# Attention of a two-layer fused kernel: both batch rows of a chunk in every operation

## The chip, the cores and the metric

One NeuronCore of a Trainium2 chip runs the whole program. The metric is the time of one execution on the device in microseconds (us); lower is better. Engines as they are named here: PE is TensorE's matrix products (PEld its weight loads), DVE is VectorE, ACT is ScalarE, POOL is GpSimd, SP is SyncE, which issues all transfers.

## What is computed

An mLSTM-like attention over 2 batch rows, 8 heads, 768 tokens and 40 channels a head; its result, 1536 tokens by 320, goes through two feed-forward layers of 2048 channels with different nonlinearities. All in fp32.

```python
for t in range(S):
    kt, vt, qt = (k[:, :, t], v[:, :, t], q[:, :, t])
    m_new = np.maximum(f_gate[:, :, t] + m, i_gate[:, :, t])
    f_stab = np.exp(f_gate[:, :, t] + m - m_new)
    i_stab = np.exp(i_gate[:, :, t] - m_new)
    m = m_new
    C = f_stab[:, :, None, None] * C + i_stab[:, :, None, None] * np.einsum('bhd,bhe->bhde', vt, kt)
    n = f_stab[:, :, None] * n + i_stab[:, :, None] * kt
    h_tilde = np.einsum('bhde,bhe->bhd', C, qt)
    denom = np.maximum(np.abs(np.einsum('bhd,bhd->bh', n, qt)[:, :, None]), 1.0)
    y[:, :, t] = 1.0 / (1.0 + np.exp(-o_gate[:, :, t])) * h_tilde / denom
x = y.transpose(0, 2, 1, 3).reshape(B * S, H * D)
h = x @ moe_w_in;   x = (h * np.clip(h + 3.0, 0.0, 6.0) / 6.0) @ moe_w_out
h = x @ moe2_w_in;  out = (h * np.tanh(np.log1p(np.exp(h)))) @ moe2_w_out
```

## The kernel before

The 768 tokens are cut into 6 chunks of 128. A *unit* is one batch row of one chunk; there are 12. For each unit `loads` brings q and k (`qke`, 416 KB) and k, v and the output gate (`kvo`, 484 KB); `scores` makes the products of q and k (tile `s`); `decays` makes the decay matrix by a scan (tile `fb`) and multiplies it with `s`; `values` scales v with the input gate and takes the gate's sigmoid; `cross` multiplies q with the carried state (`x`) and scales it into `oc`; `carry` scales k, multiplies it with v (`st`) and updates the state `c`; `within` multiplies `fb` with v (`z`, for both rows of a chunk together); the rest of `unit` adds `z` and `oc`, divides, gates, transposes (`xp`) and writes the result to X as a high part (`xh`) and a low part (`xl`). The products of attention use small tiles of the array, 40 or 64 rows by 64 columns; many stand side by side, and one run of them in PE's list is called a group below. The other products use the whole array.

Layer 1 takes the first two chunks in steps of 256 tokens (`ph`, `acc`) and the other four in blocks of 512 (`phw`, `accw`); layer 2 takes three blocks of 512 (`qh`, `bcc`). Every fp32 product is split into high and low parts. The weights arrive as `ri` and `ro` (768 and 640 KB for each of the 8 slots of a layer) and are split in `prep` by ACT and DVE or POOL; three of the `ro` slots of layer 1 have their low part made by PE instead (`low_on_pe`, tile `pw`). Until layer 1 has begun, `keep_warm` fills PE's idle time with products of zeros (`pz`).

The order on every engine is written out when the program is built: each job is a generator that asks for an engine with a duration, `Flow` plays them against one another with modelled durations and the table `P` of priorities, and the engines then run their lists in that order, each waiting in place for what an instruction needs. So an instruction that is late holds all behind it on its engine. SP's list of transfers is such a list too.

Of the kernel before, what the change touches and what calls it, by code (L numbers as in the profile page):

```python
# [8 lines left out]
F32 = mybir.dt.float32  # L9
F32R = mybir.dt.float32r  # L10
# [27 lines left out]
KVO = 2 * DM + H * E1  # L38
# [4 lines left out]
    "const": [21, 95, 223],  # L43
    "gates": [27, 37, 26, 68, 145, 320],
    "load": [17, 51, 194, 1, 24, 30, 176, 184, 28, 55, 116, 316],
    "score": [110, 40, 164, 39, 262, 141, 186, 143, 25, 248, 107, 242],
    "value": [92, 232, 149, 93, 334, 34, 284, 175, 138, 309, 342, 269],
    "carry": [330, 64, 56, 180, 231, 13, 133, 4, 229, 307, 62, 8],
    "unit": [89, 79, 57, 136, 46, 102, 70, 52, 42, 20, 169, 237],
# [8 lines left out]
    ],  # L58
    "down2": [
        244, 204, 112, 163, 183, 32, 155, 14, 78, 91, 19, 222, 33, 294, 0, 109, 29, 125, 99, 105, 211, 47,  # L60
        72, 83, 171, 63, 11, 142, 6, 202, 101, 310, 185, 77, 53, 111, 217, 224, 103, 9, 86, 22, 12, 208,
        270, 170, 333, 158,
    ],
    "wide1": [
        2, 258, 123, 289, 199, 159, 311, 61, 331, 255, 139, 167, 165, 279, 197, 131, 150, 195, 326, 118,
        250, 45, 246, 282, 203, 339, 302, 286, 278, 303, 329, 35,
    ],
    "down1w": [
        38, 193, 220, 264, 221, 7, 153, 295, 214, 124, 177, 156, 69, 65, 67, 74, 5, 36, 104, 84, 31, 117,
        114, 100, 82, 260, 73, 179, 80, 18, 173, 328,  # L70
    ],
    "drain": [59, 272, 129, 243, 43, 10, 54, 227, 238, 182],
    "now": [15, 16],
    "window": [0.05],
    "on_value": [0, 1, 1, 0, 1, 1, 2, 1, 1, 2, 1, 1],
    "on_key": [0, 0, 1, 2, 1, 0, 1, 2, 0, 2, 1, 1],
    "on_gate": [1, 0, 0, 0, 0, 2, 2, 0, 1, 2, 1, 0],
    "pool_state": [1, 0, 0, 1, 0, 1, 1, 0, 0, 0, 0, 0, 0, 0, 0, 0, 0, 0, 1, 0],
# [4 lines left out]
        0, 0, 0, 0, 0, 0, 0, 1, 0, 0, 1, 0, 1, 1, 1, 1, 1, 0, 0, 0, 0, 1, 1, 1, 1, 0, 0, 1, 0, 0, 0, 0, 1,  # L83
        0, 0, 0, 0, 0, 0, 0, 1, 1, 0, 0, 0, 1, 1, 0,
# [3 lines left out]
    "pe_low": [0, 1, 0, 0, 0, 0, 0, 0, 0, 0, 0, 0],  # L88
    "spread": [1, 1, 0, 0, 0, 0],
    "decay": [189, 134, 290, 137, 144, 308, 325, 283, 174, 120, 96, 313],  # L90
    "gload": [257, 178, 198, 48, 90, 298, 201, 41, 148, 287, 98, 128],
    "cross": [196, 162, 296, 172, 66, 200, 50, 181, 267, 241, 280, 2],
    "within": [315, 140, 317, 3, 304, 230],
    "on_cross": [0, 0, 0, 0, 0, 0, 0, 0, 0, 1, 0, 0],
# [7 lines left out]
FBS = 4  # L102


def make_consts():
    import numpy as np

    c = np.zeros((B * H, CW), np.float32)
    for r in range(B * H):
        b, h = divmod(r, H)  # L110
        p, g = divmod(h, 4)
        c[r, 64 * p : 64 * p + D] = 1.0
        c[r, CM + b * 4 + g] = 1.0
    return c
# [27 lines left out]
class Flow:  # L142
# [5 lines left out]
    TICK, COLUMNS = 10.24 / 3, 4000  # L148

# [85 lines left out]
    def transfer(self, place, t, size, n, issue):  # L235

        rate = 15e3 if t < 10 else 18.5e3
        for i in range(n):
            self.rings[i] = max(self.rings[i], t + 1.0) + size / n / rate
        end = max(self.rings[:n]) + 0.25  # L240
# [57 lines left out]
def mlstm_mlp_kernel(ctx, tc, qk, kvon, gates_io, w1i, w1o, w2i, w2o, eyes, consts, out):  # L298
# [21 lines left out]
    apool = att_stack.enter_context(tc.tile_pool(name="apool", bufs=2))  # L320
# [10 lines left out]
    in_fb, in_qke, in_kvo, in_rc, in_gp, in_fz, in_pr = (Slots(n) for n in (FBS, 2, 2, 2, 1, 1, 1))  # L331
    in_oc = [Slots(2), Slots(1)]
# [106 lines left out]
    for j in range(len(BLOCKS)):  # L439
        X.append((xpool.tile([128, 3, 512], F32R, tag=f"xh{j}", name=f"xh{j}"),  # L440
                  xpool.tile([128, 3, 512], F32R, tag=f"xl{j}", name=f"xl{j}")))
# [222 lines left out]
    def gates(c):  # L664
# [49 lines left out]
        yield PE, 0.25, 40  # L714
        T.matmul(pf[:QP, 256:272], cst[:, 0:QP], dd.rearrange("r g a -> r (g a)"), start=True, stop=True, skip_group_check=True)
        T.matmul(pf[:, 272:280], pr, ident[:16, 0:8], start=True, stop=True, skip_group_check=True)
        for a in range(2):
            T.matmul(pf[64 - 64 * a : 128 - 64 * a, 280:288], pr[:, a * HL : (a + 1) * HL], ident[:16, 8:16],
# [4 lines left out]
        yield DVE, 0.07  # L723
        V.tensor_copy(prefix[c], pf[:, 272:288])
        yield DVE, 0.07
# [625 lines left out]
```

## Time and profile before

| | |
|---|---|
| median of 3 runs | 444.06 us (443.64 to 445.39) |
| the profiled execution, its own time | 446.41 us |
| its span, first to last instruction | 444.6 us |
| busy: PE, DVE, ACT, POOL | 433.0, 303.4, 282.6, 67.6 us |
| instructions: DVE, ACT, POOL | 598, 552, 67 |
| moved by the transfers | 39.28 MB |

The span and what lies around it (1.8 us) make the profiled execution's own time, and this was 2.35 us over the median of the runs. PE's busy time counts overlapping products whole and counts the products of zeros, so a busy PE is not a useful one: below, the time of a product is read from its start to the start of the next.

### The profile page before, as it was taken

The numbers are of one execution on the slowest core, as the hardware profiler recorded it, in microseconds if no ns is written. First come the engines' busy times: TensorE is split into PE (matmuls) and PEld (weight loads), VectorE is DVE, ScalarE is ACT, GpSimd is POOL, SyncE is SP. The second block draws the span as 40 slices with busy tenths as digits, with TensorE's granted clock in tenths as the row PEclk, the third lists the DMA queues.
The fourth block names the chain that finished last, engine by engine and source line by source line (L and its number), as shares of the span: only waits on it lengthen the run. The fifth ranks groups of instructions, "written<-read, shape, count | busy, mean of one in ns | idle before, by whom it ended". The sixth has DMA issues, their size and how long they took to land.

```text
span 444.6 us, 9247 instructions
## 1 busy us (share of the span) xinstructions
PE 433.0 (97%) x3768; PEld 373.0 (84%) x3768; DVE 303.4 (68%) x598; ACT 282.6 (64%) x552; POOL 67.6 (15%) x67
## 2 busy tenths in 40 slices
PE   7999998999999999999999999999999999999995
PEld 5778797999997787888788888999998998989994
DVE  3889999797476653658786537766656666566674
ACT  3358785449358444369778448766767666666763
POOL 2114004534211025101325010000000000000000
PEclk9999999899999999999999999999999999999998
DMA  7957759344131328007352000000020000100002
GB/s 212 329 167 234 242 192 306 83 136 131 39 93 45 88 68 310 1 9 260 135 161 99 1 0 2 0 1 0 0 60 1 1 0 1 53 8 0 2 0 59
DMA packets 12118, 39.28 MB, mean 88 GB/s; under 512 B 2444, under 2 KB 4140, under 8 KB 12076
## 3 DMA queue, kind: packets, MB, share of 16 engines
q1 hardware_dynamic: 12076, 38.70, 27.3%
q8 instruction: 29, 0.48, 0.5%
q14 instruction: 13, 0.11, 0.1%
HBM read 36.46 MB, written 2.23 MB: 87 GB/s over the span
## 4 chain that ended last, share of the span: by engine, by line
PE 80%; DVE 7%; ACT 6%; DMA 3%; issue 1%; SPq 0%; ACTq 0%; DVEq 0%
PE qh L457 15%; PE accw L474 14%; PE phw L457 13%; PE acc L474 7%; PE ph L457 6%; PE bcc L1155 5%; PE bcc L1154 5%; PE bcc L1153 5%; PE pz L1186 2%; PE s L813 2%; DVE u L1098 2%; PE z L983 1%; PE x L894 1%; DMA ro<-in_w1o 1%; PE st L945 1%; ACT u L1100 1%
## 5 line engine op out<-in xcount | busy, mean ns | idle before, releaser
L1155 PE MATMUL bcc<-wd,gl 128*128 128x320 f32 x192 | 59.6, 311 | 0.5 <-DVE gl L1110 0.5
L1153 PE MATMUL bcc<-wd,gh 128*128 128x320 f32 x192 | 59.5, 310 | 0.1
L1154 PE MATMUL bcc<-wd,gh 128*128 128x320 f32 x192 | 59.3, 309 | 0.0
L457 PE MATMUL qh<-xl,wh 128*128 128x512 f32 x144 | 56.6, 393 | 0.0
L457 PE MATMUL qh<-xh,wh 128*128 128x512 f32 x144 | 56.5, 392 | 0.0
L1104 DVE SCALAR_TENSOR_TENSOR u<-u,qh 128x512 f32<-128x512 f32 (+1 forms) x49 | 33.1, 675 | 33.4 <-ACT u L1102 33.4
L1100 ACT ACTIVATE u<-u,two 128x512 f32<-128x512 f32 (+1 forms) x49 | 35.0, 715 | 31.8 <-DVE u L1098 31.8
L474 PE MATMUL accw<-ghw,wd 128*128 128x512 f32 x160 | 53.8, 401 | 0.0
L541 DVE SCALAR_TENSOR_TENSOR rw<-rw,phw 128x512 f32<-128x512 f32 x32 | 21.9, 685 | 24.3 <-ACT rw L539 24.2
L1153 PEld LDWEIGHTS bcc<-wd,gh 128*128 128x128 f32 x192 | 36.1, 188 | 2.8 <-ACT gh L1108 0.9
L1110 DVE SCALAR_TENSOR_TENSOR gl<-u,gh 128x512 fp32r<-128x512 f32 (+1 forms) x49 | 33.1, 675 | 7.8 <-ACT gh L1108 7.7
L474 PE MATMUL accw<-glw,wd 128*128 128x512 f32 x96 | 38.1, 397 | 0.0
L457 PE MATMUL phw<-xh,wh 128*128 128x512 f32 x96 | 37.9, 395 | 0.0
L457 PE MATMUL qh<-xh,wl 128*128 128x512 f32 x96 | 37.9, 394 | 0.0
L457 PE MATMUL phw<-xl,wh 128*128 128x512 f32 x96 | 37.6, 392 | 0.0
L1154 PEld LDWEIGHTS bcc<-wd,gh 128*128 128x128 f32 x192 | 36.1, 188 | 1.8
L1094 ACT ACTIVATE u<-qh 128x512 f32<-128x512 f32 (+1 forms) x49 | 28.5, 584 | 14.0 <-PE qh L457 14.0
L1155 PEld LDWEIGHTS bcc<-wd,gl 128*128 128x128 f32 x192 | 36.1, 188 | 1.3 <-DVE gl L1110 1.3
L474 PEld LDWEIGHTS accw<-ghw,wd 128*128 128x128 f32 x160 | 29.4, 188 | 6.5
L1098 DVE SCALAR_TENSOR_TENSOR u<-u 128x512 f32<-128x512 f32 (+1 forms) x49 | 33.4, 681 | 1.6
L474 PE MATMUL acc<-gh,wd 128*128 128x256 f32 x160 | 34.4, 298 | 0.0
L539 ACT ACTIVATE rw<-phw,half 128x512 f32<-128x512 f32 x32 | 22.0, 688 | 18.5 <-PE phw L457 17.9
(163 smaller groups left out, 994.8 us busy)
## 6 DMA issues: line engine op xcount, KB each, us to landing
ri<-in_w1i SPq DMA_DIRECT2D x8, 768.0 KB, 8.6
ri<-in_w2i SPq DMA_DIRECT2D x8, 768.0 KB, 8.7
kvo<-in_kvon SPq DMA_DIRECT2D x12, 484.0 KB, 5.3
ro<-in_w1o SPq DMA_DIRECT2D x8, 640.0 KB, 10.9
ro<-in_w2o SPq DMA_DIRECT2D x8, 640.0 KB, 5.8
qke<-in_qk SPq DMA_DIRECT2D x12, 416.0 KB
fb<-fzd SPq DMA_DIRECT2D x8, 256.0 KB, 3.4
out<-ot SPq DMA_DIRECT2D x6, 160.0 KB, 1.9
```

Source lines behind the costliest of these rows:

```text
L457: T.matmul(ph, a, b, start=(i == 0), stop=(i == len(seq) - 1))
L474: T.matmul(acc[k], a, b, start=start, stop=stop, skip_group_check=True)
L539: A.activation(r, ph, AF.Relu, bias=half, scale=1.0 / 6.0)
L541: V.scalar_tensor_tensor(out=r, in0=r, scalar=1.0, in1=ph, op0=ALU.min, op1=ALU.mult)
L1094: A.activation(u, ph, AF.Exp)
L1098: V.scalar_tensor_tensor(out=u, in0=u, scalar=2.0, in1=u, op0=ALU.add, op1=ALU.mult)
L1100: A.activation(u, u, AF.Ln, bias=two)
L1104: V.scalar_tensor_tensor(out=u, in0=u, scalar=0.5, in1=ph, op0=ALU.subtract, op1=ALU.mult)
L1110: V.scalar_tensor_tensor(out=gl, in0=u, scalar=-2.0, in1=gh.bitcast(F32), op0=ALU.mult, op1=ALU.subtract)
L1153: T.matmul(acc, a, hi, start=st, stop=False)
L1154: T.matmul(acc, a, lo, start=False, stop=False)
L1155: T.matmul(acc, b, hi, start=False, stop=sp)
```

## The change

A chunk's two rows are handled together. The host lays the inputs out by chunk, with the 16 heads of both rows side by side; `loads` brings one `qke` (832 KB) and one `kvo` (968 KB) a chunk; `scores`, `carry` and `cross` each issue the products of both rows in one group; the elementwise operations take 16 heads in one instruction (8 where a tile of PSUM ends). Buffers: `qke` and `kvo` have one slot each in place of two (chunks 1 and 3 keep their `kvo` in the space of the third X tile), `fb` has two of double width, and `oc` one. `scaled` now uses DVE or POOL, no longer ACT. Table `P` is new throughout, and `Flow`'s model of a transfer has other constants. The counts of products, of feed-forward instructions and of bytes stay the same.

```diff
-KVO = 2 * DM + H * E1
+KVO = B * (2 * DM + H * E1)
...
-    "score": [110, 40, 164, 39, 262, 141, 186, 143, 25, 248, 107, 242],
+    "score": [9, 84, 243, 262, 211, 292],
...
-FBS = 4
+FBS = 2
+R = B * H
...
-    apool = att_stack.enter_context(tc.tile_pool(name="apool", bufs=2))
+    apool = att_stack.enter_context(tc.tile_pool(name="apool", bufs=1))
...
-    in_fb, in_qke, in_kvo, in_rc, in_gp, in_fz, in_pr = (Slots(n) for n in (FBS, 2, 2, 2, 1, 1, 1))
-    in_oc = [Slots(2), Slots(1)]
+    in_fb, in_qke, in_kvo, in_x2, in_oc, in_gp, in_fz, in_pr = (Slots(n) for n in (FBS, 1, 1, 1, 1, 1, 1, 1))
...
+        t["qke"] = apool.tile([QP, B, 2, 4, L], F32, tag="qke", name=f"qke{c}")
+        yield SP, 852e3, ev["qk"], 13, 0.54
+        SY.dma_start(out=t["qke"], in_=qk[c])
+        t["ring"] = in_x2 if c in (1, 3) else in_kvo
+        yield t["ring"]
...
+        yield SP, 992e3, ev["kvo"]
+        SY.dma_start(out=kvo[:, 0:KVO], in_=kvon[c * L : (c + 1) * L])
...
+    def scaled(on, x, scale, n):
+        yield flow.elementwise(on, 0.07 + R * n / 960, R * n)
+        tt(G if on else V, x, x, scale.unsqueeze(2).to_broadcast([128, R, n]), ALU.mult)
+
+    def quads(first=0):
+        for a in range(first, 2):
+            for p in range(2):
+                yield a, slice(a * HL, (a + 1) * HL), p, slice(64 * p, 64 * p + D)
+
+    def scores(c):
...
+        yield PE, 0.95, 2048, 1
+        for b in range(B):
+            for h in range(4):
+                cols = slice((b * 4 + h) * HL, (b * 4 + h + 1) * HL)
+                for a, z, p, r in quads():
+                    x = t["qke"][r, b]
+                    T.matmul(sp[p][z, cols], x[:, 1, h, z], x[:, 0, h, z], start=True, stop=True, skip_group_check=True)
+        flow.set(done[c]["s"])
...
+        for b in range(B):
+            for h in range(4):
+                g = b * 4 + h
+                for a, z, p, r in quads(0 if c else 1):
+                    out = slice(64 * (a ^ b), 64 * (a ^ b) + 64)
+                    T.matmul(x[p][out, g * E1 : (g + 1) * E1], t["qke"][r, b, 0, h, z], states[2 * c + a][r, g, :],
+                             start=True, stop=True, skip_group_check=True)
+        flow.set(done[c]["cross"])
...
+        yield done[c]["s"]
+        flow.put(in_qke)
...
+        yield PE, 0.95, 1312, 1
+        for b in range(B):
+            for h in range(4):
+                g = b * 4 + h
+                for p in range(2):
+                    r = p * 8 + g
+                    w = QP - 64 if p else 64
+                    for a in range(n):
+                        z = slice(a * HL, (a + 1) * HL)
+                        T.matmul(sps[a][64 * p : 64 * p + w, g * E1 : (g + 1) * E1], kf[z, r * D : r * D + w], vi[z, r, :],
+                                 start=True, stop=True, skip_group_check=True)
...
```

What the change does to the order is seen at three places. SP's list begins, before, with the gates and the inputs of chunk 0 row by row (`qke_0`, `kvo_0`, two of each):

```order
L1170 DMA gio<-in_gates_io 16x2x128
L1172 DMA eye<-in_eyes 128x256
L762 DMA qke_0_120<-in_qk 104x1024
L1226 DMA cst<-in_consts 16x112
L769 DMA kvo_0_168<-in_kvon 128x968
L354 DMA ro_0_156<-in_w1o 128x2560
L762 DMA qke_0_176<-in_qk 104x1024
L354 DMA ri_0_157<-in_w1i 128x3072
L769 DMA kvo_0_185<-in_kvon 128x968
```

and now with four weight loads ahead of them:

```order
L357 DMA ro_1_137<-in_w1o 128x2560
L1184 DMA gio<-in_gates_io 16x2x128
L1186 DMA eye<-in_eyes 128x256
L1244 DMA gio<-in_gates_io 16x2x640
L1240 DMA cst<-in_consts 16x112
L357 DMA ro_3_138<-in_w1o 128x2560
L357 DMA ri_0_139<-in_w1i 128x3072
L357 DMA ro_0_140<-in_w1o 128x2560
L767 DMA qke_104<-in_qk 104x2048
L775 DMA kvo_158<-in_kvon 128x1936
```

The four weight loads moved ahead of chunk 0's inputs, and each input is one load of both rows; behind these rows the new list has `ri_2`, `ro_4`, `ro_2`, `ri_1`, then `qke` and `kvo` of chunk 1.

On PE, before, the products that make low weight parts (`pw`) stand between steps of layer 1 (here behind `ph_2`, the third of its steps):

```order
L391 MATMUL pw_3_320_861<-ro_3_603,eye 128x320
L392 MATMUL pw_3_320_861<-wd_3_141,minus 128x320
L671 MATMUL pg_893<-eye,gio 128x16
L672 MATMUL pg_893<-eye,gio 128x16
L391 MATMUL pw_4_320_901<-ro_4_738,eye 128x320
L392 MATMUL pw_4_320_901<-wd_4_138,minus 128x320
```

and now all six pairs stand ahead of layer 1's first step, among the products of zeros; four of them are these:

```order
L1200 MATMUL pz<-zeros 128x512
L394 MATMUL pw_4_320_539<-ro_4_318,eye 128x320
L395 MATMUL pw_4_320_539<-wd_4_122,minus 128x320
L394 MATMUL pw_2_320_547<-ro_2_328,eye 128x320
L395 MATMUL pw_2_320_547<-wd_2_113,minus 128x320
L1200 MATMUL pz<-zeros 128x512
L394 MATMUL pw_4_320_559<-ro_4_318,eye 128x320
L395 MATMUL pw_4_320_559<-wd_4_122,minus 128x320
L394 MATMUL pw_2_320_564<-ro_2_328,eye 128x320
L395 MATMUL pw_2_320_564<-wd_2_113,minus 128x320
```

They moved from inside layer 1 to the time before it. The last is what PE does right ahead of the first product of layer 1 (`ph_0`). Before, it is the scores of one row of chunk 1 and filling:

```order
L813 MATMUL s_1_0_582<-qke_1_364 64x64
L813 MATMUL s_1_1_583<-qke_1_364 64x64
L1186 MATMUL pz<-zeros 128x512 x2
L457 MATMUL ph_0_610<-xh_93,wh_0_127 128x256
L457 MATMUL ph_0_610<-xl_94,wh_0_127 128x256
```

Now it is chunk 1's products of k and v, of both rows, behind the scores of both:

```order
L942 MATMUL st_0_643<-kvo_532 64x41
L942 MATMUL st_1_644<-kvo_532 64x41
L942 MATMUL st_0_643<-kvo_532 40x41
L942 MATMUL st_1_644<-kvo_532 40x41
L465 MATMUL ph_0_680<-x_93,wh_0_108 128x256 x2
```

So layer 1 now begins behind all that chunk 1's `st` waits for, its `kvo` among it.

## Rows read from the trace of the kernel before


**Rows 1.** Windows by stage: us, busy time of each engine (instructions), granted clock, DMA share, GB/s.

```profile
0.00:35.10 35.10, 32.01 (x462) 24.47 (x463) 23.60 (x67) 15.83 (x34) 6.55 (x16) 1.00 0.76 239
35.10:82.20 47.10, 44.30 (x563) 39.10 (x561) 41.78 (x102) 33.77 (x82) 12.47 (x12) 0.96 0.71 232
82.20:190.00 107.80, 107.80 (x1469) 93.41 (x1469) 72.35 (x165) 59.53 (x155) 31.10 (x27) 1.00 0.31 97
190.00:444.60 254.60, 248.92 (x1280) 216.02 (x1278) 165.72 (x268) 173.52 (x283) 17.50 (x12) 1.00 0.12 37
```

**Rows 2.** Timeline around layer 1's first product: start, us, engine, line, operation.

```profile
19.18 2.35 PE L1186 MATMUL pz<-zeros 128*128 128x512 f32 x9
...
35.14 0.28 PE L457 MATMUL ph<-xh,wh 128*128 128x256 f32 x1
...
35.26 1.09 ACT L362 CAST top<-ri 128x768 f16<-128x768 bf16 x1
```

**Rows 3.** Timeline of PE at its only long wait ahead of layer 2.

```profile
72.93 0.28 PE L457 MATMUL ph<-xl,wh 128*128 128x256 f32 x1
75.18 0.69 PE L813 MATMUL s<-qke 40*64 40x64 f32 x32 [1.97 <-DVE dd L305]
```

**Rows 4.** The window behind that wait, columns as in rows 1.

```profile
77.00:80.50 3.50, 3.50 (x19) 3.28 (x17) 1.43 (x4) 1.14 (x3) 2.44 (x3) 0.51 0.82 246
```

**Rows 5.** Timeline of PE around groups of small-tile products.

```profile
88.20 0.28 PE L457 MATMUL ph<-xh,wh 128*128 128x256 f32 x1
88.32 0.28 PE L457 MATMUL ph<-xl,wh 128*128 128x256 f32 x1
88.53 0.68 PE L894 MATMUL x<-c,qke 40*64 40x41 f32 x32
89.14 0.39 PE L457 MATMUL ph<-xh,wh 128*128 128x256 f32 x1
89.36 0.28 PE L457 MATMUL ph<-xl,wh 128*128 128x256 f32 x1
...
93.00 1.14 PE L983 MATMUL z<-kvo,fb 64*64 64x41 f32 x64
94.07 0.50 PE L474 MATMUL acc<-gh,wd 128*128 128x256 f32 x2
```

**Rows 6.** Timeline of PE at one `pw` pair.

```profile
48.52 0.83 PE L391 MATMUL pw<-ro,eye 128*128 128x320 f32 x2
...
49.34 0.28 PE L457 MATMUL ph<-xh,wh 128*128 128x256 f32 x1
```

**Rows 7.** Windows of the first 40 us, columns as in rows 1.

```profile
0.00:10.00 10.00, 7.67 (x72) 5.48 (x74) 3.08 (x15) 3.49 (x10) 2.96 (x10) 1.00 0.70 208
10.00:20.00 10.00, 10.00 (x144) 7.94 (x141) 7.56 (x16) 4.61 (x8) 1.16 (x2) 1.00 1.01 338
...
30.00:40.00 10.00, 9.11 (x104) 7.79 (x101) 9.72 (x15) 7.50 (x15) 4.29 (x5) 1.00 0.81 265
```

**Rows 8.** Timeline: v of chunk 0's second row is scaled.

```profile
18.85 0.74 POOL L305 TENSOR_TENSOR kvo<-kvo,ist 128x328 f32<-128x328 f32 x1
```

**Rows 9.** DVE by line and shape: count, busy us, mean ns, idle ahead.

```profile
L305 DVE TENSOR_TENSOR fb<-fb,s 128x256 f32<-128x256 f32 x24 | 9.2, 411 | 0.2
L305 DVE TENSOR_TENSOR wl<-ri,wh 128x512 fp32r<-128x512 f32 x11 | 7.6, 688 | 0.8 <-ACT wh L402 0.6
```

**Rows 10.** Timeline of DVE: its longest wait in the second stage.

```profile
81.17 0.18 DVE L724 COPY px<-pf 128x16 f32<-128x16 f32 x1 [2.74 <-PE pf L718]
```

**Rows 11.** Transfers as the page lists them: KB each, us from issue to landing.

```profile
ri<-in_w1i SPq DMA_DIRECT2D x8, 768.0 KB, 8.6
...
kvo<-in_kvon SPq DMA_DIRECT2D x12, 484.0 KB, 5.3
ro<-in_w1o SPq DMA_DIRECT2D x8, 640.0 KB, 10.9
```

More of the change, by code (lines that the diff above doesn't have):

```diff
@@ L148 @@
     TICK, COLUMNS = 10.24 / 3, 4000
+    DMA = dict(rings0=2.0, slow=13e3, fast=20e3, until=3.0, start=1.9, end=0.5)
     def __init__(self):
@@ L235, in transfer @@
     def transfer(self, place, t, size, n, issue):
-        rate = 15e3 if t < 10 else 18.5e3
+        d = self.DMA
+        rate = d["slow"] if t < d["until"] else d["fast"]
         for i in range(n):
-            self.rings[i] = max(self.rings[i], t + 1.0) + size / n / rate
-        end = max(self.rings[:n]) + 0.25
+            self.rings[i] = max(self.rings[i], t + d["start"]) + size / n / rate
+        end = max(self.rings[:n]) + d["end"]
         self.landed.append(end)
@@ L838, in decays @@
-        yield (DVE, 1.135) if P["spread"][c] else (DVE, 1.135, True)
-        V.tensor_tensor_scan(out=f2, data0=fin, data1=ident8, initial=0.0, op0=ALU.mult, op1=ALU.add)
-        if P["spread"][c]:
-            flow.put(in_h)
-        yield ACT, 0.1
-        A.copy(t["ul"], f2.rearrange("p (h t) -> p h t", h=H)[:, :, HL - 1 : HL])
-        flow.set(done[u]["ul"])
-        yield done[u]["s"]
-        for p in range(2):
-            yield DVE, 0.33
-            part = f2[:, p * 256 : (p + 1) * 256]
-            tt(V, part, part, t["s"][p][:, 0:256], ALU.mult)
+        else:
+            yield got[c]["f"]
@@ new lines, in decays @@
+        for p in range(2):
+            part = fin = f[:, p * 512 : (p + 1) * 512]
+            if spread:
+                yield in_h
+                fin = bank(f"fb{c}_{p}")
+                yield PE, 0.95, 2048, 2
+                for r in range(8):
+                    col = istab[c][:, p * 8 + r : p * 8 + r + 1].to_broadcast([128, HL])
+                    for a in range(2):
+                        z = slice(a * HL, (a + 1) * HL)
+                        T.matmul(fin[z, r * HL : (r + 1) * HL], col, identz[:, z], start=True, stop=True, skip_group_check=True)
+            yield (DVE, 1.135) if spread else (DVE, 1.135, True)
+            V.tensor_tensor_scan(out=part, data0=fin, data1=ident8, initial=0.0, op0=ALU.mult, op1=ALU.add)
+            if spread:
+                flow.put(in_h)
@@ new lines, in mixture @@
+        port = (True,) * (2 - len(parts))
+        for o, r, _ in parts:
+            yield (DVE, 0.08) + port
+            V.tensor_scalar(out=r, in0=o[..., D : D + 1], scalar1=1.0, scalar2=None, op0=ALU.max)
+            yield (DVE, 0.08) + port
+            V.scalar_tensor_tensor(out=r, in0=o[..., D : D + 1], scalar=-1.0, in1=r, op0=ALU.mult, op1=ALU.max)
+        yield DVE, 0.17
+        V.reciprocal(out=rc, in_=rc)
+        yield from scaled(P["on_gate"][c], so, rc, D)
+        for o, _, g in parts:
+            yield (DVE, 0.74 if len(parts) == 1 else 0.41) + port
+            tt(V, g, o[..., 0:D], g, ALU.mult)
+            flow.put(in_a if port == () else in_fb)
@@ new lines, in mixture @@
+        y = so.rearrange("p (q b h) d -> p q b (h d)", q=2, b=B)
+        tail = t["tail"].rearrange("p (b x) -> p b x", b=B)
+        for x in range(2):
+            yield ACT, 0.15
+            A.copy(tail[:, :, 64 * x : 64 * x + 64].rearrange("p b (q d) -> p q b d", q=2), y[:, :, :, 128:160])
+        for b in range(B):
+            i = 2 * c + b
+            yield in_a
+            xp = bank(f"xp{b}_{c}")
+            yield PE, 0.32, 1536
+            for k, part in enumerate((y[:, 0, b, 0:128], y[:, 1, b, 0:128], tail[:, b, :])):
+                T.matmul(xp[:, k * 128 : (k + 1) * 128], part, ident, is_transpose=True, start=(k == 0), stop=(k == 2),
+                         skip_group_check=True)
+            if c // 2 == len(X):
+                yield ends[3]
+                new_x()
+            xcol = ((c % 2) * 2 + b) * L
+            xh, xl = (z[:, :, xcol : xcol + L] for z in X[c // 2])
+            ps = xp[:, 0:384].rearrange("p (k t) -> p k t", k=3)
+            yield ACT, 0.37
+            A.copy(xh, ps)
+            if P["pe_low"][i]:
+                yield have["minus"]
+                yield PE, 0.18, 384
+                T.matmul(ps, minus, xh, start=False, stop=True, skip_group_check=True)
+                yield ACT, 0.36
+                A.copy(xl, ps)
+            else:
+                yield DVE, 0.47
+                sub(xl, ps, xh.bitcast(F32))
+            flow.put(in_a)
+            flow.set(x1[c][b])
@@ L1240, in scan_rest, with after_attention @@
             yield from scan_gates(i, *SCANS[i])
-    def after_attention(waits, last):
+    def after_attention(waits):
         for e in waits:
```

481 lines of the change are left out of this document (201 added, 280 removed), and 14 rows, old and new, of the table P.

## The prediction, as put on record before the changed kernel ran

> **What bounds the kernel now.** I read the windows by stage first. From 82.2 us on PE is busy 107.80 of 107.80 us and then 248.92 of 254.60 [rows 1], at a granted clock of 1.00; the missing 5.7 us are the passage between the layers and the tail, whose order the change does not touch. Between 35.1 and 82.2 PE is busy 44.30 of 47.10 us at a clock of .96. Ahead of that its 32.01 busy us are mostly products of zeros. The timeline gives the border: the first product of layer 1 starts at 35.14, right behind filling [rows 2]. So the kernel's time is a sum of three things: when layer 1 starts, how long PE's list is from there, and what PE loses on the way. Savings on DVE, ACT or POOL count only through the first and the third.
>
> What PE loses from 35.1 to 82.2 is 2.8 us of idle time and a clock effect of 47.1 × .04 = 1.9, together 4.7. The timeline shows where: behind the product at 72.93, PE has nothing until 75.18, since it waits for DVE [rows 3], and from 77.0 to 80.5 its granted clock is .51, that is 1.2 GHz in place of 2.4 [rows 4].
>
> **PE's list from the start of layer 1.** A group of 32 small products shows its fixed cost between whole-array products [rows 5]. From one `ph` product to the next is .12 us (88.20 to 88.32). The last one ahead of the group takes .21 (to 88.53), so the entry costs .09. The first behind it takes .22 (89.14 to 89.36) and so costs .10 more. The group of 32 lasts .61 and the `z` group of 64 lasts 1.07, so 32 products cost .46 and .15 is fixed. A group that is merged into another thus saves .09 + .10 + .15 = .34. I counted the groups in both orders from layer 1's start: 32 before, 17 after. Those 15 give 5.1 us; if entry and exit were hidden by something else, the .15 alone gives 2.3. Three groups' worth of products, one of `s` and two of `st`, moved ahead of the start: 3 × .46 = 1.4. Six `pw` pairs moved ahead too; one takes .82 (48.52 to 49.34, three records) [rows 6], so 6 × .82 = 4.9. Feed-forward products are the same in number. The sum is 11.4, and 8.6 with groups at .15 each. I take 11.0, near the top, because entry and exit costs stand in plain sight around nearly every group of the trace.
>
> **The start of layer 1.** It needs chunk 0 finished, and now also chunk 1's `st`, which stands ahead of `ph_0` on PE. For chunk 0: the loads up to both rows' `kvo` are 4.83 MB (3.44 before, to the second row's). The first 10 us move 208 GB/s and the next 338 [rows 7]; so 2.08 MB by 10 us, the rest at 18.1 us. Before, the second row's v is scaled at 18.85 [rows 8] and layer 1 starts 16.3 later; the same distance gives 34.4. For chunk 1: 9.55 MB stand up to its `kvo`. At 338 that is 32.1 us. From 30 to 40 us the rate was 265 with a share of .81 [rows 7]; filled up, that is 327, and would make it 32.5; at 265 from 20 us on it is 35.4. I take 32.5, since the weights' loads have buffers early and stand behind one another. Then DVE scales v twice in instructions of 656 and 640 elements. 256 elements take 411 ns and 512 take 688 [rows 9], that is 1.08 ns an element, so about .84 each; the `st` group takes 1.07 and the hand-offs about .3: 3.0 in all. The start is at 35.1 to 38.4, and 35.5 is my value: +.4.
>
> These scalings were POOL's and ACT's in part. The work put on DVE is paid by its fixed costs: the merged instructions bring its list from 598 to 531, so DVE's total hardly moves.
>
> **What PE loses behind the start.** The stretch to compare is layer 1's first five steps, in which DVE has most to do; it is busy 41.78 of 47.10 us [rows 1]. In the changed order I priced DVE's 89 instructions from chunk 1's scaling of k to the multiplication in the fourth step, each by the mean of its form or by 1.08 ns an element: 38.6 us. PE's list to the same place, priced as its products run now, is 37.6. DVE's idle time in this stretch holds a wait of 2.74 us for PE [rows 10], which PE's slow clock caused; without it DVE worked 41.78 of 44.36, or 94%. At that share 38.6 take 41.1 and PE comes out 3.5 late. Before it lost 4.7: -1.2. I count no clock loss in this, since waits spread over several steps are shorter than the 2.1 us one ahead of the fall [rows 3, 4]; if the clock falls as before, 1.7 (3.5 us at half speed) comes on top.
>
> Edits that I cost at nothing: chunks 2 to 5's inputs, `oc` in one slot and the wider decays lie beside PE's full list from 82.2 on, where DVE is busy 72.35 of 107.80 [rows 1]. POOL and ACT are far from full there. If that cover fails, rival two is what happens.
>
> **Sum.** 446.41 (the profiled execution's own time) - 11.0 + .4 - 1.2 = 434.6. The profile is 2.35 over the median of the runs, so against that median I forecast 432.3.
>
> **Rivals.** *One: DVE falls behind.* Its share with that wait counted is 41.78/47.10 = 88.7%. Then the 38.6 take 43.5, PE is 5.9 late, the clock falls for 1.7 more, and DVE, late already, also holds the start at 38.4. That is 446.41 - 11.0 + 3.3 + 2.9 - 2.35 = 439.3. For it: DVE is idle for 5.3 us of these 47.1, so a further wait comes out on PE; against: merged instructions hand over half as often.
>
> *Two: one `qke` slot.* Chunk c+1's q and k may be loaded only when chunk c's `x` is done, and in PE's order `s` stands 9.1 us (chunk 2 to 3) and 8.4 us (3 to 4) of PE's work behind that `x`. A load of 832 KB would take 4.8 us by its share of the full rate; by the 8.6 us of the 768 KB of `ri` 9.3, by the 10.9 of the 640 KB of `ro` 14.2 [rows 11]. By the first nothing is late; by the second about 1 us for both, with hand-offs 433 to 435; by the last 5.1 and 5.8, which PE spends idle, and one fall of the clock, 1.7 on each: 446.6. In that stretch the transfers' share is .31 [rows 1], so the transfer has the engines to itself, which speaks for the short price; two such waits of half their size give 438. The Trainium skill, page "Trainium Kernel Development and Optimization", section "Best Practices", advises to double-buffer so that transfers lie beside computing. By that rule the change, which takes the second slot away, would lose here; the trace shows no single-slot load, and by its rows most of the load is covered by the work between.
>
> *Three, the other side: the inputs come late.* Weights stand ahead of the inputs in SP's list, and the inputs are twice as large. If the queue moved only the 208 GB/s of its first 10 us [rows 7] throughout, chunk 1's `kvo` would land at 45.9 and layer 1 start at 48.9, 13.4 after my value: 445.7. Two more loads (1.44 MB, 52.8 at this rate) have their casts on ACT ahead of the first step's activation, at 1.09 each [rows 2]: 55.0, while PE asks for it 32 products and one `x` after the start, at 53.4. That is 1.6 more: 447.3. It is slower than before by my measure from a start of 47.9 on, that is under 213 GB/s in the mean. The trace's 338 with a full queue speaks against it; the 239 of the mean to 35.1 [rows 1] counts stretches in which nothing was issued.
>
> *Four: the groups keep their cost.* If a merged group of 64 costs as much as two of 32, the 5.1 is not there: 437.4. The `z` group of 64 [rows 5] speaks against it.
>
> **How the numbers follow.** The forecast has .55: its own range is 428 (waits behind the start gone, start at 34.4) to 436.5 (start at 38.4, or 8.6 in place of 11.0, and hand-offs). Rival one has .20, two .08, four .06, three .05; better than 428 has .06. The range that holds 8 of 10 takes in the forecast, rivals one and four and the mild end of two: 427 to 441. A change of .5% (2.2 us) is what a measurement of this kernel can tell from none: faster means under 441.8, slower over 446.3. Faster: the forecast, the better case, one, four and the mild half of two, less a little for several mishaps together: .89. Slower: three and the bad end of two: .05. The rest, .06, is the same.
>
> **What would show it.** The first `ph` product starts at 35 to 36, behind an `st` group of 64 products that ran right after chunk 1's `kvo` was scaled; a start past 38 is my error in the transfers. From there, every group of small products is 64 records in about 1.07 us, with .09 ahead and .10 behind. No `pw` stands behind the first `ph`. PE's idle time between the start and 80 us is 3 to 4 us and names DVE, and no stretch has a clock near .5; one that has is rival one. PE's waits at `s` for a `qke` transfer are rival two. The span from the first `ph` to the end is then about 397 us (now 409.5, less 11.0 and 1.2). I am wrong above all if DVE's 94% is not kept: each point of it costs .4 us of PE's time in the first steps.

## The result, and the profile after

The changed kernel takes 438.85 us (median of 13 runs, 436.98 to 441.73) where the kernel before takes 444.04 (13 runs): a ratio of .9884, with an interval of .9854 to .9913. It is faster by 5.2 us; the forecast was 11.8. The profiled execution took 441.38 us with a span of 439.6, so it lies 2.5 over its median, as the one of before did (2.35).

The windows by stage, cut at layer 1's first product and then at 82.2 and 188.0 us (columns as in [rows 1]; PE is 35 feed-forward products further on at 82.2 than it was there before, and 20 further at 188.0 than before at 190.0):

```profile
0.00:42.60 42.60, 38.41 (x589) 29.04 (x589) 31.16 (x68) 24.77 (x52) 6.76 (x15) 0.96 0.85 283
42.60:82.20 39.60, 38.46 (x485) 36.73 (x482) 37.74 (x83) 27.16 (x58) 4.28 (x3) 1.00 0.56 171
82.20:188.00 105.80, 105.44 (x1448) 92.00 (x1447) 70.05 (x118) 42.05 (x80) 27.53 (x21) 1.00 0.35 105
188.00:439.60 251.60, 245.68 (x1265) 212.32 (x1263) 165.42 (x266) 175.05 (x285) 21.24 (x15) 1.00 0.12 37
```

Layer 1 starts at 42.63, not at 35.14 [rows 2] and not at 35.5 as forecast. From there to the end it is 396.97 us in place of 409.46; the forecast was 397.3. In the second row PE is idle for 1.14 us at a clock of 1.00, where it lost 4.7 before [rows 1]. So what was to be saved behind the start was saved, and 7.1 of it were spent ahead of the start.

PE's timeline, and SP's, on the way to that start:

```profile
25.09 0.66 PE L890 MATMUL x<-c,qke 40*64 40x41 f32 x20
27.74 0.55 PE L890 MATMUL x<-c,qke 40*64 40x41 f32 x12 [1.99 <-issue]
28.22 3.86 PE L1200 MATMUL pz<-zeros 128*128 128x512 f32 x9
...
32.01 1.15 PE L985 MATMUL z<-kvo,fb 64*64 64x41 f32 x64
...
36.81 1.16 PE L815 MATMUL s<-qke 40*64 40x64 f32 x64
...
41.58 1.13 PE L942 MATMUL st<-kvo 64*64 64x41 f32 x64
42.63 0.50 PE L465 MATMUL ph<-x,wh 128*128 128x256 f32 x2
...
18.07 0.33 SPq L357 DMA_DIRECT2D ri<-in_w1i  x1
28.32 0.33 SPq L767 DMA_DIRECT2D qke<-in_qk  x1
28.70 0.36 SPq L775 DMA_DIRECT2D kvo<-in_kvon  x1
```

Three things are to be seen. PE stops in the middle of chunk 0's `x`, behind its 20th product, for 1.99 us; "issue" means that it waits for nothing in the records. The load of chunk 1's q and k is issued at 28.32, as soon as `x` is done, since there is one slot; for 10 us before that SP issued nothing. And the nine products of zeros behind `x` take .43 us each, against .26 in [rows 2]: the granted clock is at 1.2 GHz for part of them (.61 in the mean from 28.30 to 29.90, the last row below).

The transfers of that time: what SP issued at 5.2 to 6.6 us, then at 28.2 to 29.0 (KB, us from issue to landing), and two windows, with clock, DMA share and GB/s at the end:

```profile
kvo<-in_kvon SPq DMA_DIRECT2D x1, 968.0 KB, 14.8
...
kvo<-in_kvon SPq DMA_DIRECT2D x1, 968.0 KB, 9.6
...
25.90:29.20 3.30, 1.46 (x15) 1.27 (x15) 1.11 (x4) 1.70 (x3) 2.04 (x2) 0.92 0.03 12
28.30:29.90 1.60, 1.60 (x5) 1.26 (x6) 1.52 (x5) 0.00 (x0) 0.00 (x0) 0.61 0.38 77
```

Chunk 0's `kvo` lands at 5.96 + 14.8 = 20.8 (forecast 18.1), chunk 1's at 28.70 + 9.6 = 38.3 (forecast 32.5), and in between the queue is all but empty for 3.3 us (a share of .03). Where PE stopped, the transfers show a load of program code: in the .04 us from 25.28 on, a 16 KB packet of the instruction queue starts, the only one of this size from 20.35 to 27.75.

```profile
q8 instruction: 1, 0.02, 166.9%
```

DVE ahead of the start (timeline), and its merged operations by shape, which answer to [rows 9]:

```profile
33.20 0.91 DVE L309 TENSOR_TENSOR fb<-z,oc 128x328 f32<-128x328 f32 x2 [2.08 <-PE z L985]
...
38.70 1.29 DVE L309 TENSOR_TENSOR fb<-fb,s 128x512 f32<-128x512 f32 x2
39.90 0.83 DVE L309 TENSOR_TENSOR kvo<-kvo,ist 128x656 f32<-128x656 f32 x1
40.66 0.82 DVE L309 TENSOR_TENSOR kvo<-kvo,ul 128x640 f32<-128x640 f32 x1
...
L309 DVE TENSOR_TENSOR fb<-fb,s 128x512 f32<-128x512 f32 x12 | 7.9, 679 | 0.0
L309 DVE TENSOR_TENSOR kvo<-kvo,ul 128x640 f32<-128x640 f32 x5 | 4.1, 814 | 1.3 <-DMA kvo<-in_kvon 1.3
```

The durations are as forecast (.84 for 640 elements; .69 for 512). But the scaling stands in DVE's list behind the multiplications with `s`, so from `s` at 36.81 to the first product it is 5.8 us.

These rows also tell which chain held the start in this execution. DVE waits for chunk 0's `z` until 33.20 and from there works without a gap of more than .26 us to the end of the scalings at 41.48; from 33.20 to the start it is 9.4 us. Chunk 1's `kvo` has landed at 38.3 and is taken up at 39.90, when DVE comes to it, and `s` waits for nothing. So neither load of chunk 1 held the start here: chunk 0 did, with PE's stop and the slow products of zeros ahead of `z`. The wait of 1.3 us for `kvo` in the last row is chunk 3's, at 104.16, and PE did not wait then.

### The profile page after: what moved, and what is told of

The parts are those of the page before. It is cut to its first block, busy times and chain, and to the rows that moved or that the text cites. A ratio compares the mean times of both kernels' runs of the same rounds, so it can differ in the third digit from the quotient of the medians.

```text
span 439.6 us, 9071 instructions
## 1 busy us (share of the span) xinstructions
PE 428.0 (97%) x3779; PEld 370.1 (84%) x3779; DVE 304.4 (69%) x532; ACT 269.0 (61%) x472; POOL 59.8 (14%) x54
## 4 chain that ended last, share of the span: by engine, by line
PE 76%; DVE 9%; DMA 6%; ACT 3%; issue 3%; POOL 1%; SPq 0%; DVEq 0%; POOLq 0%; ACTq 0%
PE qh L465 20%; PE accw L482 10%; PE phw L465 10%; PE bcc L1169 6%; PE bcc L1168 6%; PE bcc L1167 6%; PE pz L1200 4%; PE ph L465 3%; PE acc L482 3%; DMA kvo<-in_kvon 2%; DMA fb<-fzd 1%; DVE ri L367 1%; PE x L890 1%; DMA ro<-in_w2o 1%; PE fb L840 1%
## 5 line engine op out<-in xcount | busy, mean ns | idle before, releaser
L465 PE MATMUL qh<-x,wh 128*128 128x512 f32 x288 | 89.5, 392 | 0.0
L465 PEld LDWEIGHTS qh<-x,wh 128*128 128x128 f32 x288 | 52.3, 188 | 8.7
L465 PE MATMUL phw<-x,wh 128*128 128x512 f32 x192 | 58.9, 394 | 0.0
L465 PEld LDWEIGHTS phw<-x,wh 128*128 128x128 f32 x192 | 35.7, 188 | 8.1
L465 PE MATMUL qh<-x,wl 128*128 128x512 f32 x96 | 37.9, 395 | 0.0
L482 PEld LDWEIGHTS accw<-ghw,wd 128*128 128x128 f32 x160 | 29.5, 188 | 6.7 <-ACT ghw L552 0.5
L465 PE MATMUL ph<-x,wh 128*128 128x256 f32 x192 | 34.2, 288 | 0.0
```

The costliest lines, as they stand in the source:

```text
L465: T.matmul(ph, a, b, start=(i == 0), stop=(i == len(seq) - 1))
L482: T.matmul(acc[k], a, b, start=start, stop=stop, skip_group_check=True)
```

## The experiments

The theory to be tested, in two parts. One: the start is late because chunk 1's q and k wait for chunk 0's `x`. Two: PE's stop inside `x` is the end of a 16 KB piece of its program, whose successor stands behind data in the transfers. The rivals: chunk 0's `kvo` is late, or PE's own list (the products of zeros, `pw`) holds the start. Each experiment keeps all lists of the changed kernel but for the edit named. A ratio is to runs of the kernel before that were taken beside it, so ratios are to be compared, not medians; a start is that of one profiled execution, and it varies: lists that are the same up to there gave 42.63 and 41.10 (the groups cut, below). A further rival, DVE's list behind chunk 0's `z`, is varied by none of them.

**A place of its own for chunk 1's q and k.**

```diff
-        t["qke"] = apool.tile([QP, B, 2, 4, L], F32, tag="qke", name=f"qke{c}")
+        if c == 1:
+            q1 = xpool.tile([128, 3072], F32, tag="x1", name="qke1")
+            t["qke"] = q1[0:QP, 0 : B * 8 * L].rearrange("p (b i h t) -> p b i h t", b=B, i=2, h=4)
+        else:
+            t["qke"] = apool.tile([QP, B, 2, 4, L], F32, tag="qke", name=f"qke{c}")
```

> Chunk 1's q and k get a place of their own (the space of the second X tile), so their load need not wait for chunk 0's x; all lists stay as they are. In the changed kernel the load was issued at 28.32, right behind x (28.28), and layer 1 began at 42.63 in place of 35.5 as forecast. If the single slot is what makes the start late: the load is issued at about 18.4, chunk 1's kvo lands by 32, the start is at 36 to 39, and the time about 434. If the rest of chunk 0 (x late by a 2.0 us wait of PE for its program code, then nine products of zeros at the low clock, z, the pw pairs) holds the start as well: 41.5 to 42.6 and 438. If PE's code is loaded behind the data in the transfer queue, the wait in x grows, since the queue now stays full: start up to 45 and 441.

444.14 us, ratio to before .9971 (.9939 to 1.0003): all the gain is gone. PE's timeline and two windows; then what SP issued from 19.7 to 20.9 us:

```profile
26.15 0.66 PE L894 MATMUL x<-c,qke 40*64 40x41 f32 x20
32.38 0.87 PE L894 MATMUL x<-c,qke 40*64 40x41 f32 x12 [5.57 <-issue]
...
48.34 0.50 PE L465 MATMUL ph<-x,wh 128*128 128x256 f32 x2
...
20.00:26.80 6.80, 6.43 (x183) 5.15 (x176) 6.43 (x13) 3.06 (x5) 0.00 (x0) 1.00 1.02 389
26.80:32.40 5.60, 0.03 (x4) 0.01 (x2) 0.39 (x1) 1.88 (x3) 2.04 (x2) 0.91 0.89 185
...
kvo<-in_kvon SPq DMA_DIRECT2D x1, 968.0 KB, 15.8
```

The third expectation came true, and more: PE stops at the same product for 5.57 us. Its code, one 16 KB packet, starts only at about 29.5, while the queue is full of chunk 1's inputs. The last row shows a second thing: issued 8 us earlier (20.49), `kvo` lands at 36.3, only 2 us earlier. In the second window the transfer engines are busy for .89 of the time and move 185 GB/s; in the first, mostly weights, 389. The inputs are slower per byte than the weights.

**Chunk 0's inputs ahead of three weights** (the two loads are moved behind `cst` in SP's list).

```diff
         SY.dma_start(out=cst, in_=consts)
...
+        SY.dma_start(out=first_in["qke"], in_=qk[0])
...
+        SY.dma_start(out=first_in["kvo"][:, 0:KVO], in_=kvon[0:L])
```

> Chunk 0's qke and kvo are loaded ahead of ro_3, ri_0 and ro_0 in place of behind them; nothing else moves. If the late landing of chunk 0's kvo (20.77 us, forecast 18.1) is the cause: it lands near 14, x ends 3 to 5 us earlier, the start is near 39 and the time 435. If it is not: the three weights land later by 1.84 MB, about 7 us, DVE and ACT have them ahead of chunk 0's scores in their lists, and the start stays at 42 to 43, the time at 438 to 439.

444.52 us, .9982 (.9948 to 1.0015). DVE's timeline:

```profile
16.42 0.83 DVE L367 SCALAR_TENSOR_TENSOR ro<-ro,top 128x640 uint32<-128x640 uint32 x1 [6.40 <-ACT top L365]
```

DVE waited 6.40 us for the weights that now come later and has them ahead of chunk 0 in its list; `s` of chunk 0 began at 25.27 in place of 18.30, and layer 1 at 46.23. Late by more than the second expectation. Since the weights held up chunk 0 itself, the run shows that this order is worse, and not what the late landing of chunk 0's `kvo` costs; that rival stays untested.

**The nine products of zeros left out.**

```diff
         def fill():
-            T.matmul(pz, zeros[:, 0:128], zeros, start=True, stop=True)
+            count[0] += 1
+            if not 43 < count[0] <= 52:
+                T.matmul(pz, zeros[:, 0:128], zeros, start=True, stop=True)
```

> The nine products of zeros between chunk 0's x and z (28.22 to 32.0 us, at .43 each since the granted clock was at 1.2 GHz) are left out; they are in no result. If PE's list ahead of layer 1 holds the start, z begins at 28.4 and the start is 3 to 3.7 earlier, near 39, time 435.5. If the load of chunk 1's q and k, issued at 28.32 behind x, holds it as well, s begins no earlier than 35.5 and the start gains at most 1.3: 41.3 to 42.6, time 437.5 to 439.

438.61 us, .9828 (.9784 to .9872), which overlaps the changed kernel's interval. PE's timeline:

```profile
27.84 0.43 PE L890 MATMUL x<-c,qke 40*64 40x41 f32 x9 [1.18 <-issue]
...
35.77 1.16 PE L815 MATMUL s<-qke 40*64 40x64 f32 x64 [1.39 <-DMA qke<-in_qk]
...
41.20 0.50 PE L465 MATMUL ph<-x,wh 128*128 128x256 f32 x2
```

`z` comes 3.8 earlier (28.19), but `s` then waits for the load of q and k, and the start is 1.4 earlier: the second expectation. Two chains of nearly the same length lead from `x` to the start, one through zeros, `z` and DVE's list behind it, one through that load. The 1.4 itself is not to be put down to the edit, since unchanged lists gave a start of 41.10.

**ri_1 loaded behind chunk 1's inputs.**

```diff
-        SY.dma_start(out=raw[:, 1 : size + 1].rearrange("p (k s) -> p k s", k=k), in_=src.bitcast(U16))
+        def load():
+            SY.dma_start(out=raw[:, 1 : size + 1].rearrange("p (k s) -> p k s", k=k), in_=src.bitcast(U16))
+
+        if name == "i0_1":
+            held.append(load)
+        else:
+            load()
...
         SY.dma_start(out=kvo[:, 0:KVO], in_=kvon[c * L : (c + 1) * L])
+        if c == 1:
+            held.pop()()
```

> The load of ri_1 (768 KB), issued at 18.07 us, moves behind chunk 1's kvo; nothing else moves. In the changed kernel PE stood still inside chunk 0's x from 25.75 to 27.74 and waited for nothing in the records, while 16 KB of program code were loaded from 25.78 on, just as the weights' last packets went out. If that load stood behind the data: the engines run dry some 2 us earlier, the 16 KB are loaded by 24, x has no wait, ends near 26.3 and the clock does not fall behind it. If the wait is one of PE's own, it is there again with some 2 us. The start itself gains little either way, since ri_1 then lands near 37 and is ahead of chunk 1's decays in DVE's list: 41 to 43, time 437 to 440.

445.50 us, .9997 (.9968 to 1.0026). PE's timeline, then DVE's:

```profile
27.08 0.55 PE L899 MATMUL x<-c,qke 40*64 40x41 f32 x12 [0.92 <-issue]
...
42.18 0.66 PE L1050 MATMUL xp<-eye,kvo 128*128 128x128 f32 x2 [5.72 <-DVE kvo L309]
...
40.34 0.96 DVE L374 SCALAR_TENSOR_TENSOR ri<-ri,top 128x768 uint32<-128x768 uint32 x1 [6.88 <-ACT top L372]
```

The stop is .92, shorter, but not gone (the code packet of the changed kernel, put at 25.78 above, starts at 25.3 by the window shown). It says little: with unchanged lists up to there it was 1.18 and .92 in two other runs (the nine zeros left out; the groups cut, below). The start, at 48.66, was much later than expected: DVE waits 6.88 us for ri_1 and has the end of chunk 0 behind it.

**The first 20 products of zeros left out**, so that the program's pieces end 40 instructions further on.

```diff
-            T.matmul(pz, zeros[:, 0:128], zeros, start=True, stop=True)
+            count[0] += 1
+            if count[0] > 20:
+                T.matmul(pz, zeros[:, 0:128], zeros, start=True, stop=True)
```

> The first 20 products of zeros (1.3 to 7.7 us; in no result) are left out, so that every later product of PE stands 40 instructions earlier in its program (each product is a weight load and a product). So far PE always stood still at the same place, behind the 20th product of chunk 0's x: 1.99 us in the changed kernel, 5.57 with the second q/k load queued ahead, .92 with ri_1 out of the queue. If this is the end of a 16 KB piece of program whose successor waits behind data: x loses its wait, since the end is now 40 instructions later, in the products of zeros behind x; x ends near 26.4, chunk 1's q and k are issued then, and the start comes 1 to 2 earlier: 40.5 to 41.5, time 437 to 438. If the wait belongs to x (its operands, a bank): it stays behind the 20th product with 1 to 2 us, and the start at 42 to 43.

438.22 us, .9879 (.9832 to .9926). PE's timeline:

```profile
26.34 0.93 PE L890 MATMUL x<-c,qke 40*64 40x41 f32 x32
...
35.56 1.17 PE L815 MATMUL s<-qke 40*64 40x64 f32 x64 [1.21 <-DMA qke<-in_qk]
...
41.02 0.50 PE L465 MATMUL ph<-x,wh 128*128 128x256 f32 x2
```

All 32 products of `x` run in one piece: the stop did not belong to `x` but to its place in the program. The later runs without both sets of zeros show where it went: in four of the five PE stops behind the eighth product of `z`, 20 products or 40 instructions further on. The start is 1.6 earlier in this profile, which unchanged lists reach too (41.10); the time is not to be told from the changed kernel's.

**The groups cut in two** behind the start (the edit in `scores`; alike in `cross` and `carry`).

```diff
         for b in range(B):
+            if b and c > 1:
+                T.matmul(sp[0][:, 4 * HL : 4 * HL + 40], jmat, jmat[:, 0:40], start=True, stop=True, skip_group_check=True)
```

> Behind layer 1's start each of 13 groups of 64 small products (5 of x, 4 of s, 4 of st) is cut in two by one whole-array product of 40 columns, written where the second half's first products write over it. By the prediction's terms each cut costs .09 + .10 + .15 and the product itself some .03: .37 each, 4.8 in all, so that the stretch from layer 1's first product to the end grows from 396.97 to about 401.5 and the time by 4 to 5. If entry and exit of a group cost nothing of PE's time there, it grows by .4 (the products alone); at .15 each by 2.3.

444.13 us, 1.0003 (.9971 to 1.0035): with every merged group cut, the changed kernel is no faster than before. PE's timeline at one `x`:

```profile
44.17 0.68 PE L894 MATMUL x<-c,qke 40*64 40x41 f32 x32
44.77 0.29 PE L889 MATMUL x<-jmat 128*128 128x40 f32 x1
44.99 0.68 PE L894 MATMUL x<-c,qke 40*64 40x41 f32 x32
45.60 0.50 PE L465 MATMUL ph<-x,wh 128*128 128x256 f32 x2
```

It takes 1.43 from its start to the next `ph`, where the 64 uncut products of the changed kernel took 1.07 (45.70 to 46.77). The stretch from the first product to the end is 400.5; over the twelve other profiles of the changed kernel's lists it is 394.3 to 397.0, mean 395.8. So 13 cuts cost 4.7, or .36 each, as expected (3.5 to 6.2, or .27 to .48 each, against the ends of that spread).

Up to the start this run's lists are the changed kernel's, so it also shows what an execution does without any edit:

```profile
27.66 0.55 PE L894 MATMUL x<-c,qke 40*64 40x41 f32 x12 [0.92 <-issue]
28.14 2.33 PE L1206 MATMUL pz<-zeros 128*128 128x512 f32 x9
30.40 1.14 PE L991 MATMUL z<-kvo,fb 64*64 64x41 f32 x64
...
35.66 1.16 PE L817 MATMUL s<-qke 40*64 40x64 f32 x64 [0.38 <-DMA qke<-in_qk]
...
41.10 0.50 PE L465 MATMUL ph<-x,wh 128*128 128x256 f32 x2
```

`x` began a microsecond later (26.08), but PE goes on behind its stop at 27.66, where it was 27.74 in the changed kernel's profile. The granted clock does not fall (1.00 from 26 to 42 us), the nine products of zeros take 2.3 in place of 3.8, and the start is 1.5 earlier: the slow zeros are the difference between the two executions.

**Zeros left out in both places**, and **with the second place** on top (edits as above).

> Both the first 20 and the nine products of zeros between chunk 0's x and z are left out. If code, filling and the single q/k slot are the three parts of the late start: x ends near 26.4, z follows at 27 to 28, chunk 1's q and k are issued at 26.5 and land near 34, s starts at 34 and layer 1 at 39 to 39.5, time 435 to 436. If filling and code had been hidden by something else: 41 as with the filling alone left out, time 438.

> The same, and chunk 1's q and k in a place of their own, so that their load is queued at about 18.5 again. If the code stands behind data, PE stands still 40 instructions later than with the second place alone, that is inside z: until 30 to 32, so x ends at 26.5 but z only at 32 to 34; then q, k and v are there and the start is at 39 to 42, time 436 to 439. If the second place had been slower for another reason (the input's transfers taking weights' time), the wait in z is under 1 us and the start still past 42.

The first: 439.91 us, .9908 (.9872 to .9944), start at 41.30; `x` without a stop, q and k issued at 27.09, `s` at 34.89 behind a wait of 1.56 for them. That is the second expectation: `s` came early, but behind that wait the granted clock was .53 from 36.3 to 39.9, and the products between `s` and `st` went slowly. The second: 441.89 us, .9916 (.9883 to .9950). Its profiled execution was the fastest of its twelve, with the earliest start seen, 39.51; PE's timeline and chunk 1's `kvo`, issued at 20.38:

```profile
27.16 1.03 PE L989 MATMUL z<-kvo,fb 64*64 64x41 f32 x56 [0.32 <-issue]
...
34.87 0.35 PE L819 MATMUL s<-qke 40*64 40x64 f32 x9 [0.85 <-issue]
...
39.51 0.50 PE L465 MATMUL ph<-x,wh 128*128 128x256 f32 x2
...
kvo<-in_kvon SPq DMA_DIRECT2D x1, 968.0 KB, 14.7
```

With q and k early and short stops, the start is 3.1 earlier than in the changed kernel's profile. It is DVE's list that sets it now: from chunk 0's `x` (27.03) to the end of chunk 1's scalings (38.06) DVE has no gap of more than .26 us, and chunk 1's `kvo`, landed at 35.1, is taken up at 36.49. That profile does not stand for the median: in most other executions of this kernel the mean granted clock was .983 to .994 (here .999) and the time 439 to 444.

**Three other ways to bring the inputs earlier**, all without the 29 products of zeros but the third: chunk 1's `kvo` issued ahead of its `qke`; the second place with its load held until the first state is copied, by this one-column copy on ACT; the same hold alone.

```diff
                 A.copy(new, add)
+                A.copy(gate[0][:, 1:2], gate[0][:, 0:1])
```

> On top of the kernel without the 29 products of zeros, chunk 1's kvo, which waits for nothing, is issued ahead of chunk 1's qke in place of behind it (near 19 in place of 27.5 us). If what is left of the late start is that both inputs are loaded only behind chunk 0's x: qke, alone now, lands 5 to 6 us after its issue at 27 in place of 8, s starts near 33 and layer 1 near 38.5 to 39, time 434 to 436. If the longer queue holds PE's program code: a wait without a releaser in z or s of 1 to 4 us, start 39 to 42 and 436 to 440.

> On top of the kernel without the 29 products of zeros, chunk 1's q and k have a place of their own, but their load is held until chunk 0's first carried state is copied (near 25 us), by a one-column copy on ACT that reads the place; so the queue runs nearly dry ahead of it, as before, and the load no longer waits for x. If single slot and code are the parts: issue at 25 to 25.5, landing near 33, s near 33, layer 1 at 38.5 to 39.3, time 434 to 436, and the runs lie closer together than with the second place alone (438 to 447). If the order of DVE holds the start whatever the inputs do: 41, and 438.

> The same held second place in the changed kernel as it is, with all its products of zeros. The code's end is inside x again, so x waits for 1 to 2.5 us there, but the load no longer waits for x; z stands behind nine products of zeros at 30 to 32 and the pw pairs behind it. If the filling is hidden once the inputs come earlier: 39 to 40 and 436. If PE's list takes over as the bound: s at 35.5 to 36.5, the start at 41 to 42, 438.

439.81 us (.9897, .9862 to .9932), 439.43 (.9886, .9837 to .9936) and 439.40 (.9898, .9842 to .9954). PE's timeline in the first, then in the second:

```profile
29.84 1.03 PE L990 MATMUL z<-kvo,fb 64*64 64x41 f32 x56 [2.91 <-issue]
...
36.63 0.50 PE L819 MATMUL s<-qke 40*64 40x64 f32 x9 [1.70 <-issue]
```

The first stopped for 2.91 us in `z`, start 42.11: the expectation with code. The other two did not do what they were meant to: the copy came late on ACT, so the load was issued at 26.52 and 27.17, some 1 us ahead of `x`'s end; with starts at 42.36 and 41.57 they leave the question open.

**Second place, `kvo` held** (without the 29 products of zeros; the same copy holds `kvo` in place of `qke`).

> As the run with the second place and without the 29 products of zeros, but only chunk 1's q and k are queued early; its kvo is held until chunk 0's first carried state is copied (near 26 us), so 968 KB less stand in the queue while chunk 0 is worked on. If the program code behind data is what spoils the second place: waits without a releaser in z and s sum to under 1.5 us (2.5 there), s starts at 32.5 to 33.5, layer 1 at 39 to 39.5, the clock does not fall, and the median is 436 to 438 with less spread than 438 to 447. If kvo is then too late: it lands at 33 to 34, behind s, and costs nothing up to 35; later than that the start is at 40 to 41 and the time 438 to 439.

441.63 us, .9911 (.9877 to .9946). PE's timeline:

```profile
32.93 1.74 PE L990 MATMUL z<-kvo,fb 64*64 64x41 f32 x56 [5.11 <-issue]
```

Wrong: with less data queued than in the run with both inputs early, the stop in `z` was 5.11 in place of .32, and the start 44.73. Its code packet started at about 30.1.

## Why the prediction was partly right

**What bounds the kernel: right.** The time is the start of layer 1 plus PE's list plus what PE loses. In all kernels with these lists the stretch behind the start is 394 to 397 us (400.5 with the groups cut), while the start moves from 39.5 to 48.7 and the profiled time with it.

**PE's list: right in its terms.** Cutting 13 groups costs .36 each, of which some .03 is the inserted product by the estimate made before the run, where the prediction had .34 and its lower bound .15; no `pw` stands behind the start. Rival four (groups keep their cost) is out. By the windows, the stretch is 12.5 shorter: 3.6 come from lost time in the first steps (4.7 to 1.1) and .6 are given back behind 82.2 (idle .36 and 5.92, before 0 and 5.68), which leaves 9.5 for the list, inside the 8.6 to 11.4 but under the 11.0 taken. Where the 1.5 went was not traced.

**What PE loses behind the start: right in sign, too small.** 1.1 in place of 3.5, one wait of PE for DVE:

```profile
54.76 0.39 PE L482 MATMUL acc<-gl,wd 128*128 128x256 f32 x1 [1.14 <-DVE gl L309]
```

The clock did not fall. DVE was busy for 37.74 of 39.60 us, 95% where the prediction carried over 94%; at its own .4 us a point that is only .5 of the 2.4, and the rest was not traced. This 2.4 and the 1.5 of the list nearly cancel, which is why 397.3 met 396.97 so closely. Rival one (DVE falls behind) is out.

**The start of layer 1: the step that failed.** The start was 42.63 in place of 35.5, and both of the prediction's terms for it were too small.

The term for chunk 0: "Before, the second row's v is scaled at 18.85 [rows 8] and layer 1 starts 16.3 later; the same distance gives 34.4." In the changed kernel v is scaled at 20.81, 2.7 later than worked out, and the start is 21.8 behind it, 5.5 more than was carried over from the old order. From `z` to the start it is 10.6 now and was 10.5 before (`z` at 24.66). The rest lies between the scaling and `z`, 11.2 us where it was 5.8: there stand PE's stop of 1.99 for code and nine products of zeros, 3.8 us and most of it at the low clock. With 2.7 and 5.5 more, 34.4 becomes 42.6; this chain held the start in the profile. The run with the groups cut shows that 1.5 of it is the low clock, which came in one execution and not in the other.

The term for chunk 1: "I take 32.5, since the weights' loads have buffers early and stand behind one another." `kvo` landed at 38.3. One part is the slot: the load stood behind chunk 0's `x`, and the queue was all but empty for 3.3 us; this is rival two's mechanism, which the prediction priced only between chunks 2, 3 and 4, where PE waits for no load now (chunk 3's `s` starts at 100.37, 7.4 us after its load was issued, so that rival's 9.3 and 14.2 are out there; its 4.8 is shown by no run). The other is the rate: even queued at 20 us, with the engines busy, `kvo` lands at 35.1 to 36.3 (second place with and without zeros), about 3 us late, since the inputs move 185 GB/s in a stretch where the transfer engines are busy for .89; the 327 came from a window in which weights were loaded too. The 3.0 from landing to start were too little as well: the scalings cost what was forecast, but wait behind `s` in DVE's list, and it was 4.3. This chain alone gives a start of about 41: 41.20 and 41.02 in the two runs with the clock up where DVE waited for an `s` that waited for the load (without the nine zeros, and without the first 20). So "a start past 38 is my error in the transfers" is half true. Rival three (the inputs come late) had the direction, not the size: its `kvo` landed at 45.9.

Behind both stands what the prediction did not add up: DVE's list ahead of the start. In the execution with the earliest start it runs from chunk 0's `x` at 27.03 to the end of chunk 1's scalings without a wait worth naming, and the start is 39.51, still 4 us after the forecast. No run shortens this list, so what it is worth alone stays open.

Put into the sum, the measured start gives 446.41 - 11.0 + 7.5 - 1.2 = 441.7; the profile took 441.38. So the 11.8 were 7.1 too many by this one term; that leaves 4.7, and the profiles differ by 5.0, the medians by 5.2.

**The rule of the Trainium skill.** With one slot the kernel did not lose, it is faster than before (.9884), though `s` waited for the load in several runs (1.39, 1.21 and 1.56 us); a second place by itself took the ratio to .9971, with PE's longest stop for code. The Trainium skill, page "Trainium Kernel Development and Optimization", section "Best Practices", advises to double-buffer. These runs bear that out by half.

**What is shown of the code, and what not.** Shown: the stop belongs to a place in the program. With 40 instructions fewer ahead of it `x` has none, and it is met again 40 instructions further on, in `z`. From one stop to the next PE goes through some 127 products and their weight loads (20.31 to 25.75 in the changed kernel). And PE goes on 2.3 to 2.9 us after a 16 KB packet of the instruction queue has started (25.3 to 27.74, 29.5 to 32.38, 30.1 to 32.93), in all 23 stops of .3 us or more that lie within the first 60 us of the changed kernel and the experiments (three others, .3 to .5 us ahead of a group near 110 us, have no such packet by them). So a stop lasts as long as the packet is late. That it starts late because it stands behind data is supported by 5.57 against .55 to 1.99 at the same product, but not settled: the last run had less queued than the one with both inputs early and stopped for longer. What decides it within a full queue stays open.

The best version stays open too: of twelve kernels none is clearly faster than the changed one; the nearest, without the nine zeros, has .9828 against .9884 with overlapping intervals.

## What to carry to other kernels

Work out a start from the lists of the new order, engine by engine, and not from a distance carried over from the old one: 16.3 us became 21.8 here. When a change takes a second buffer away, follow its first use too: the load was issued 10 us after the one ahead of it, and in the first 40 us little hid that, while in the steady part PE waited for no load. Work out a landing time from the rate of that kind of transfer, and with the queue as the changed list leaves it, gaps included, not from a rate of another mix. Merging groups of small products paid about what the single switch in the trace said, some .33 us each. An early start of a load can cost more than it brings, as the second place did. And before 1.5 us of a profile are credited to an edit, see what unchanged lists do: here they gave starts 1.5 us apart.

## What was not expected of the hardware

PE ran out of program: the 64 products of a merged group and their 64 weight loads take 1.1 us, so a 16 KB piece lasts only some 5 us in this stretch (20.31 to 25.75), and PE stood still for .3 to 5.6 us at its end while nothing in its records held it. In the changed kernel's profile the stop of 1.99 us was followed by a low clock that cost 1.5 more; with a stop of .92 the clock stayed at 1.00. With the transfer engines busy for .89 of the time the inputs moved 185 GB/s; a stretch of mostly weights moved 389 at a share of 1.02.
